# Reordering the first pair of batches in a fused retention and low-rank mixer kernel

## The chip, the core and the metric

The kernel runs on one core of a Trainium2 chip. The metric is the device time of one execution in microseconds (us). The kernel before takes 326.05 us, the median of six runs between 325.9 and 327.28.

## What is computed

First comes a retention layer (attention with decaying weights instead of a softmax), then a mixer on its output: a low-rank mixing over the sequence (U and V) and a two-layer network over the channels (w_ch1 and w_ch2). There are 8 batches, 8 heads, 576 positions, 64 channels per head, 512 channels per position.

```python
scores = scale * np.matmul(q, k.transpose(0, 1, 3, 2))
gamma = 1.0 - 2.0 ** (-5.0 - np.arange(H))
rel = pos[:, None] - pos[None, :]
Dmat = np.where(rel >= 0, gamma[:, None, None] ** rel[None, :, :], 0.0)
attn = np.matmul(scores * Dmat[None], v)
x = attn.transpose(0, 2, 1, 3).reshape(B, S, H * D)
u = x + (x.transpose(0, 2, 1) @ U @ V).transpose(0, 2, 1)
out = u + np.maximum(u @ w_ch1, 0.0) @ w_ch2
```

Inputs and output are float32 in DRAM; the matmuls run in bfloat16.

## The kernel before

Batches go in four pairs. A pair has 2 times 576 positions, which is nine chunks of 128 positions; the chunk in the middle (J, number 4) is half one batch and half the other. The decay is split into a factor on the keys and values and one on the queries or the result, so that within a chunk only a triangular mask is left, and what earlier positions contribute is kept in a running state (keys times values). The mixer then works by batch, on four or five chunks: `MA` (times U), `MH` (times V, added to x, gives u), `MT` (transposes u), Y1 (times w_ch1, ReLU, sixteen items f of 128 hidden channels) and Y2 (times w_ch2, plus u, stored).

Pairs 1 to 3 are worked chunk by chunk in `section`, laid between the Y1 and Y2 matmuls of the batch before by `merge`, which places items by a share of the summed cost. Their queries and keys are transposed by DMA (`xbar`, L279), their staging loads are issued on SyncE by `load` (L243), with 15 staging buffers in rotation.

Pair 0 is worked apart, in an order written out by hand, in `startup` (L909) and `first_stretch` (L1033). The tile framework is told to keep the program order on each engine (`tc.manual_schedule()`), so each engine does its instructions in the order in which these functions emit them, and waits by semaphores. Here the positions are taken in four units of 256 (units 0 and 1 are batch 0, units 2 and 3 are batch 1) and two half chunks J of 64 positions (`hj[0]` and `hj[1]`). The steps are:

- `load_u` (L605) and `load_J` (L792) load on SyncE; `zero_J` (L781) clears staging buffers of the half chunks first. `scale_u` (L637) and `cast_u` (L630) scale and cast to bfloat16, mostly on GpSimd; `cast_J` (L799) and `prep_vJ` (L814) do this for a half chunk: in the kernel before the keys of half chunk 0 on ScalarE and its queries, which are multiplied by `posJ`, on VectorE.
- `T_u` (L646) and `T_J` (L820) transpose on TensorE against the identity, with copies out of PSUM on ScalarE or VectorE.
- `SC_u` (L675), `SC_off` (L719) and `SC_J` (L836) are the scores of a unit, of the off-diagonal block of unit 0, and of a half chunk. `mask_u` (L690) and `mask_J` (L852) multiply by the mask on VectorE; `SC_off` has its copy on ScalarE (L730).
- `RV_u` (L701), `RV_off` (L733), `RV_J` (L862) multiply by the values. `ST_u` (L760) sums the state into `acc1` or `acc2` in PSUM; `Sblk` (L770) copies it into a slot of `sblk` on ScalarE; `QS_u` (L744) and `QS_J` multiply the queries by it. `XS_u` (L752) writes the result x on VectorE.
- `warm` (L205) runs matmuls on the identity whose result is not used.
- `load_w1` (L212) and `load_w2` (L217) load and cast the weights by DMAs issued on GpSimd. A small memset on VectorE into w2's tile (L1089) holds the eight w2 loads until it is done.

PSUM has one buffer each of the kinds `ps_sc`, `ps_o` and `ps_s`, and three `ps_big`, so that a step also waits for the reader of the tile that had its buffer before.

`early_consts` (L117) makes masks, positions and the identity. `first_stretch` lays single Y1 items of batch 0 (`y(1)`) between the steps of units 2 and 3.

Of the kernel before, what the change touches and what calls it, by code (L numbers as in the profile page):

```python
# [34 lines left out]
def kernel(  # L35
# [81 lines left out]
    def early_consts():  # L117
        scratch = y1_pool.tile([P, NF, 4 * P], BF16, tag="y10", name="y1")
        un[0]["off"] = scratch[:, 0:4, :].rearrange("p (a x) (y i) -> p a (x y) i", x=2, i=P)
        tri = scratch[:, 4, 0:P]  # L120
        make_identity(nc, ident)
        nc.gpsimd.memset(lnb, math.log(scale))
        nc.gpsimd.iota(
            posU, pattern=[[2 * P, 4], [1, 2], [0, H]], base=0, channel_multiplier=2,
            allow_small_or_imprecise_dtypes=True,
        )
        nc.gpsimd.iota(
            iotaU, pattern=[[-1, 2], [1, P]], base=0, channel_multiplier=-2,
            allow_small_or_imprecise_dtypes=True,
        )  # L130
# [13 lines left out]
        for h in range(H):  # L144
            nc.vector.memset(lngt[:, :, h], lng[h])
        nc.scalar.activation(out=Af[:, 0, 0:H], in_=lngt[:, 0, :], func=AF.Exp)
        nc.vector.tensor_copy(out=fan, in_=ident[0:R, None, 0:R].to_broadcast([R, 4, R]))
        nc.vector.tensor_scalar_add(posU[:, 2:4], posU[:, 2:4], -float(4 * P - HALF))
        nc.vector.tensor_tensor(
            out=posU.rearrange("p u j h -> p (u j) h"),  # L150
            in0=lngt[:, 0:8, :], in1=posU.rearrange("p u j h -> p (u j) h"), op=ALU.mult)
        nc.scalar.activation(out=vscaleU, in_=posU, func=AF.Exp, bias=lnb, scale=-1.0)
        nc.vector.tensor_scalar(
            out=posJ, in0=posJ, scalar1=0.5, scalar2=None, op0=ALU.mult)
        nc.vector.tensor_tensor(out=posJ, in0=posJ, in1=lngt[:, 0:2, :], op=ALU.mult)
        nc.scalar.activation(out=vscaleJ, in_=posJ, func=AF.Exp, bias=lnb, scale=-1.0)
        nc.scalar.activation(out=posJ, in_=posJ, func=AF.Exp, bias=0.0, scale=1.0)
        nc.vector.tensor_scalar(
            out=triU[0:HALF], in0=iotaU[0:HALF], scalar1=0.0, scalar2=None, op0=ALU.is_ge)
        nc.vector.tensor_scalar(  # L160
            out=triU[HALF:P], in0=iotaU[HALF:P], scalar1=-float(P), scalar2=None,
            op0=ALU.is_ge)
        nc.vector.tensor_scalar_add(pos[:, J + 1:NI, :], pos[:, J + 1:NI, :], -float(S))
        nc.vector.tensor_scalar_add(pos[HALF:P, J, :], pos[HALF:P, J, :], -float(S))
        nc.vector.tensor_tensor(out=lngt, in0=lngt, in1=pos, op=ALU.mult)
        nc.scalar.activation(out=qscale, in_=lngt, func=AF.Exp, bias=0.0, scale=1.0)
        nc.scalar.activation(out=vscale, in_=lngt, func=AF.Exp, bias=lnb, scale=-1.0)
        nc.vector.tensor_copy(out=triH[0:HALF], in_=tri[0:HALF, 0:HALF])
        nc.vector.tensor_copy(out=triH[HALF:P], in_=tri[HALF:P, HALF:P])
        nc.vector.memset(U_E[:, J, :], 0.0)  # L170
        nc.vector.memset(U_O[0:HALF, 0, :], 0.0)
        nc.vector.memset(V4[:, 0:HALF], 0.0)
        nc.vector.memset(V4[:, HALF + S:], 0.0)
        nc.vector.tensor_copy(out=swap[:, 0:HALF], in_=ident[:, HALF:P])
        nc.vector.tensor_copy(out=swap[:, HALF:P], in_=ident[:, 0:HALF])

    def load_u_rows():
        nc.sync.dma_start(
# [53 lines left out]

    ch = {}

    def load(pr, i, which):
        c = ch.setdefault((pr, i), {})
        for j in which:
            if ("f", j) not in c:
                c["f", j] = stage.tile([P, H, D], FP32, tag="stage", name="stage_t")
            dram = (q, k, v)[j]  # L240
            for rows, b, t0 in parts(pr, i):
                n = rows.stop - rows.start
                nc.sync.dma_start(  # L243
                    out=c["f", j][rows, :, :],
                    in_=dram[b, :, t0:t0 + n, :].rearrange("h s d -> s h d"),
                )
# [534 lines left out]
    def zero_J(x, eng):  # L781
        for j in range(3):
            t = stage.tile([P, H, D], FP32, tag="stage", name="stage_t")
            hj[x]["f", j] = t
            if eng is nc.scalar:
                nc.scalar.activation(
                    out=t.rearrange("p h d -> p (h d)"),
                    in_=ident[:, None, :].to_broadcast([P, 4, P]), func=AF.Copy, scale=0.0)
            else:
                eng.memset(t, 0.0)  # L790
# [6 lines left out]
                out=hj[x]["f", j][0:P:2], in_=src.rearrange("h s d -> s h d"))  # L797

    def cast_J(x, eng_k, eng_q):  # L799
        t = qk_pool.tile([P, 2, dm], BF16, tag="qk", name="qk")  # L800
        hj[x]["qk"] = t
        for j, e in ((1, eng_k), (0, eng_q)):
            f = hj[x]["f", j]
            if j == 0 and x == 0:
                e.tensor_tensor(
                    out=t[:, 0, :].rearrange("p (h d) -> p h d", d=D), in0=f,
                    in1=posJ[:, 0, :, None].to_broadcast([P, H, D]), op=ALU.mult)
            elif e is nc.scalar:
                nc.scalar.activation(
                    out=t[:, j, :], in_=f.rearrange("p h d -> p (h d)"), func=AF.Copy)  # L810
            else:
                e.tensor_copy(out=t[:, j, :], in_=f.rearrange("p h d -> p (h d)"))
# [96 lines left out]
    def startup():  # L909
# [12 lines left out]
        cast_unit(0)  # L922
        T_u(0, 1, nc.vector)
        nc.vector.memset(un[0]["off"][HI], 0.0)
        zero_J(1, nc.vector)
        load_J(1, (1, 0, 2))
        load_u(2, (1, 0, 2))
# [7 lines left out]
        cast_unit(1)  # L935
        cast_u(0, 2, 0, nc.gpsimd)
        cast_u(0, 2, 1, nc.gpsimd)
        cast_u(1, 2, 0, nc.gpsimd)
        load_w1(0, 2)
        cast_u(1, 2, 1, nc.gpsimd)  # L940
        T_u(1, 1, nc.scalar)
        SC_u(0, 1, ps_o, "po")
        mask_u(0, 1)
        SC_off(0, ps_sc, "psc")
        warm(3)
        T_u(1, 0)
        nc.vector.memset(sblk, 0.0)
        SC_off(1, ps_o, "po")
        warm(3)
        SC_u(1, 0, ps_sc, "psc")  # L950
        mask_u(1, 0)
        cast_J(0, nc.scalar, nc.vector)
        SC_u(1, 1, ps_o, "po")
        mask_u(1, 1)

        acc1 = pss_tile()
        ST_u(0, ALL, acc1, True)
        Sblk(acc1, 1)
        RV_u(0, 0)
        RV_u(0, 1)  # L960
        RV_off()
        XS_u(0)
        T_J(0)
        acc2 = ps_big.tile([P, NHP, P], FP32, tag="big", name="pss2")
        ST_u(0, ALL, acc2, True)
        prep_vJ(0)
        cast_urows()
        RV_u(1, 0)
        SC_J(0)
        mask_J(0)  # L970
        ST_u(1, LO, acc1, False)
        Sblk(acc1, 2)
        cast_J(1, nc.gpsimd, nc.gpsimd)
        load_w1(2, 4)
        prep_vJ(1)
        load_w1(4, 6)
        scale_u(2, 0, nc.gpsimd)
# [4 lines left out]
        load_w1(8, 10)  # L982
        for hh in range(2):
            cast_u(2, 2, hh, nc.gpsimd)
        load_w1(10, 14)
        scale_u(3, 0, nc.gpsimd)
        for hh in range(2):
            cast_u(3, 0, hh, nc.gpsimd)
        load_w1(14, 16)
        for hh in range(2):  # L990
            cast_u(3, 2, hh, nc.gpsimd)
        RV_u(1, 1)
        QS_u(1, 0, 1)
        XS_u(1, 0, 1)
        ST_u(1, ALL, acc2, False)
        Sblk(acc2, 3)
        QS_u(1, 1, 2)
        XS_u(1, 1, 2)
        RV_J(0)
# [33 lines left out]
    def first_stretch():  # L1033
# [3 lines left out]
        def y(n):  # L1037
            for _ in range(n):
                fn = next(ys, None)
                if fn is not None:  # L1040
                    fn()
# [13 lines left out]

        def unit(u, slots, last):
            T_u(u, 1, nc.vector)
            if last:
                y(1)
            T_u(u, 0)  # L1060
            y(1)
            SC_u(u, 0, ps_sc, "psc")
# [19 lines left out]
            XS_u(u)  # L1082

        for g in range(NI, NI + 4):
            load(*order[g], (1, 0, 2) if g < NI + 3 else (1, 0))
        unit(2, (0, 1, 2), False)
        y(2)
        unit(3, (2, 3), True)
        nc.vector.memset(w2_sb[:, 0, 0:1], 0.0)  # L1089
        for f in range(0, NF, 2):  # L1090
            load_w2(f)
        y(1)
        MA1()
# [1 line left out]
        MH1(outs1[0])  # L1095
        y(2)
        MT1(outs1[0])
        MH1(outs1[1])
        y(16)
        Y1, rest = y1_items(1, by_seg=True)  # L1100
# [68 lines left out]
```

## Time and profile before

| what | value |
|---|---|
| median of six runs | 326.05 us |
| the profiled execution | 325.9 us |
| its span, first to last instruction | 324.1 us |
| TensorE busy | 313.6 us, 97% of the span |
| VectorE, ScalarE, GpSimd busy | 174.0, 145.7, 101.3 us |
| granted TensorE clock | 0.999 |
| bytes moved | 53.3 MB, mean 164 GB/s |
| first Y1 matmul (L515) starts | 24.57 us |
| first transpose by DMA for pair 1 issued, landed | 60.27, 66.98 us |

The profile is of one execution. PE is TensorE, PEld its weight loads, DVE is VectorE, ACT is ScalarE, POOL is GpSimd, SP is SyncE, which only issues DMAs here. In the table of the span in 40 slices (8.1 us each) a digit is the busy share of a slice in tenths. The DMA share is the summed time of packets over 16 engines; since packets of two queues overlap in it, it can be above 1. A row of the timeline has the start, the duration, the engine, the line, the operation and its tiles, the count, and in brackets the idle time before it and what ended it. A line of waits has the total in us, the number of times, and the longest. Ends of matmuls are modelled, so the distance between starts of matmuls is the better measure.

### The profile page before, as it was taken

The page shows a single profiled execution, that of the slowest core. Times are in us where ns is not written, and L with a number is a line of the kernel's source. Part 1 is how long each engine was busy: PE and PEld are TensorE (multiplying, and loading weights), DVE is VectorE, ACT ScalarE, POOL GpSimd, SP SyncE. Part 2 cuts the span into 40 slices and gives each one's busy share as a digit, 9 for nine tenths or more (in the row PEclk, how much of TensorE's full clock was granted, in tenths as well). Part 3 has the DMA queues.
Part 4 walks back from the last instruction along what each step waited for, and adds up shares of the span by engine and source line. Part 5 has one row for each costly group of instructions (what it writes and reads, how often), then busy time and mean ns, then how long its engine had stood idle before and what let it go on. Part 6 is the DMA issues. An engine that isn't in the chain of part 4 may idle for free.

```text
span 324.1 us, 9143 instructions
## 1 busy us (share of the span) xinstructions
PE 313.6 (97%) x3885; PEld 171.2 (53%) x3885; DVE 174.0 (54%) x342; ACT 145.7 (45%) x334; POOL 101.3 (31%) x172
## 2 busy tenths in 40 slices
PE   8899989999999999999999999999999999999996
PEld 3575545764444444457644454457644444467544
DVE  7866546229725577556844476556744475500012
ACT  6757547892020474058800583058800572047400
POOL 7797239222113722052221523052231500010000
PEclk9999999999999999999999999999999999999999
DMA  8999989989975999969997599859997360330022
GB/s 210 262 239 260 237 183 196 208 171 126 256 187 135 244 194 186 211 155 184 192 207 159 140 188 204 215 139 179 191 214 162 97 67 4 106 106 0 2 78 84
DMA packets 152904, 53.30 MB, mean 164 GB/s; under 512 B 132032, under 2 KB 150336, under 8 KB 152864
## 3 DMA queue, kind: packets, MB, share of 16 engines
q1 hardware_dynamic: 144512, 40.40, 68.8%
q0 software_dynamic: 8352, 12.32, 15.6%
q8 instruction: 30, 0.49, 0.7%
q14 instruction: 10, 0.08, 0.1%
HBM read 36.85 MB, written 9.44 MB: 143 GB/s over the span
## 4 chain that ended last, share of the span: by engine, by line
PE 75%; ACT 4%; DMA 3%; DVE 2%; issue 1%; DVEq 0%
PE ps_y L549 35%; PE ps_y L515 32%; DMA qkT<-qk 3%; PE pp L296 2%; DVE u L464 2%; ACT y L520 2%; PE pp L316 1%; PE ps_y L560 1%; PE pp L328 1%; PE AB L358 1%; PE pa L431 1%; PE ph L458 1%; ACT s_sb L373 1%; ACT qk L264 0%; ACT uT L489 0%
## 5 line engine op out<-in xcount | busy, mean ns | idle before, releaser
L515 PE MATMUL ps_y<-uT,w_sb 128*128 128x256 bf16 (+2 forms) x768 | 133.1, 326 | 1.7 <-ACT y L520 1.0
L520 ACT ACTIVATE y<-ps_y 128x384 bf16<-128x384 f32 (+2 forms) x192 | 89.6, 490 | 96.9 <-PE ps_y L515 96.0
L549 PE MATMUL ps_y<-w_sb,y 128*128 128x512 bf16 x560 | 126.5, 380 | 0.0
L515 PEld LDWEIGHTS <-w_sb 128*128 128x128 bf16 x768 | 72.3, 98 | 49.6 <-issue 3.8
L549 PEld LDWEIGHTS <-y 128*128 128x128 bf16 x560 | 52.5, 98 | 61.2
L272 POOL TENSOR_TENSOR vt<-stage_t,vscale 64x256 bf16<-64x256 f32 (+1 forms) x81 | 50.1, 619 | 63.6 <-DMA stage_t<-in_v_dram 49.5
L538 DVE TENSOR_TENSOR o_sb<-ps_y,u 128x512 f32<-128x512 f32 (+2 forms) x38 | 25.2, 664 | 81.7 <-PE ps_y L549 79.3
L541 POOL DMA_DIRECT2D out_dram<-o_sb x31 | 17.1, 553 | 104.7 <-DVE o_sb L538 100.9
L304 DVE TENSOR_TENSOR ret<-pp,triH 128x512 bf16<-128x512 f32 x27 | 18.7, 692 | 23.4 <-PE pp L328 18.0
L464 DVE TENSOR_TENSOR u<-ph,xt 128x768 bf16<-128x768 f32 (+2 forms) x24 | 21.8, 950 | 5.9 <-PE ph L458 4.2
L437 ACT ACTIVATE a_sb<-pa 128x128 bf16<-128x128 f32 x8 | 2.2, 277 | 43.8 <-PE pa L431 43.8
L338 DVE COPY q<-qkT 64x256 bf16<-64x256 bf16 x48 | 14.2, 297 | 14.0 <-DMA qkT<-qk 13.1
L344 DVE TENSOR_TENSOR xt<-pp,qscale 128x512 bf16<-128x512 f32 x27 | 18.6, 689 | 4.7 <-PE pp L328 4.2
L263 DVE CAST qk<-stage_t 64x256 bf16<-64x256 f32 x54 | 18.8, 347 | 1.2
L383 DVE TENSOR_TENSOR s_sb<-AB,Af 64x256 bf16<-64x256 f32 x42 | 17.7, 422 | 2.1 <-ACT s_sb L378 1.5
L264 ACT ACTIVATE qk<-stage_t 128x512 bf16<-128x512 f32 x27 | 16.8, 622 | 0.0
L635 POOL CAST qk<-stage_t 128x512 bf16<-128x512 f32 x16 | 10.6, 660 | 10.8 <-DMA stage_t<-in_v_dram 5.3
L376 ACT ACTIVATE Af<-AB 128x256 f32<-128x256 f32 x24 | 9.2, 384 | 8.2 <-PE AB L358 7.7
L692 DVE TENSOR_TENSOR ret<-psc,triU 128x1024 bf16<-128x1024 f32 x8 | 9.6, 1206 | 3.9 <-PE psc L684 3.9
L296 PEld LDWEIGHTS <-qkT 64*64 64x64 bf16 x432 | 5.6, 107 | 10.4 <-issue 7.8
L261 ACT ACTIVATE qk<-stage_t 128x256 bf16<-128x256 f32 x27 | 11.1, 410 | 0.0
L209 PE MATMUL pw<-ident 128*128 128x512 bf16 x26 | 8.6, 477 | 1.4 <-POOL ident masks.py:199 1.4
(134 smaller groups left out, 220.1 us busy)
## 6 DMA issues: line engine op xcount, KB each, us to landing
stage_t<-in_k_dram SPq DMA_DIRECT2D x32, 256.0 KB, 4.7
stage_t<-in_q_dram SPq DMA_DIRECT2D x32, 256.0 KB, 5.5
stage_t<-in_v_dram SPq DMA_DIRECT2D x32, 256.0 KB, 5.6
out_dram<-o_sb POOLq DMA_DIRECT2D x31, 256.0 KB, 3.5
w_sb<-in_moe_w_ch_dram POOLq DMA_DIRECT2D x14, 256.0 KB, 8.1
stage_t<-in_k_dram SPq DMA_DIRECT2D x8, 128.0 KB, 3.8
stage_t<-in_q_dram SPq DMA_DIRECT2D x8, 128.0 KB, 3.9
stage_t<-in_v_dram SPq DMA_DIRECT2D x8, 128.0 KB, 4.1
```

Source lines behind the costliest of these rows:

```text
L263: nc.vector.tensor_copy(out=o[to, hl], in_=f[fr, hl])
L264: nc.scalar.activation(out=c["qk"][:, 0, :], in_=c["f", 0].rearrange("p h d -> p (h d)"), func=AF.Copy)
L272: nc.gpsimd.tensor_tensor(out=o[to, hl], in0=f[fr, hl], in1=w[fr, hl, :, None].to_broadcast([n, NHP, D]), op=ALU.mult)
L304: nc.vector.tensor_tensor(out=ret.rearrange("p a b i -> p a (b i)").rearrange("p a (b i) -> p a b i", i=D), in0=pp[:, :, 0:NHP * D].rearra ...
L344: nc.vector.tensor_tensor(out=st["x", pr][:, i, :].rearrange("p (hp hl d) -> p hl hp d", hl=2, d=D), in0=pp[:, :, NHP * D:2 * NHP * D].rea ...
L383: nc.vector.tensor_tensor(out=S_[half(x), 1, :], in0=Bk[half(1 - x)], in1=Af[half(1 - x), now, :], op=ALU.add)
L464: nc.vector.tensor_tensor(out=st["u", par][:, i0 - base:i0 - base + n, w].rearrange("p s (c d) -> p c s d", c=2), in0=ph[k][:, :, 0:n, :], ...
L515: nc.tensor.matmul(ps[:, 0:n, :], w1_sb[:, cc, f * P:(f + 1) * P], st["uT", par][:, c0:c0 + n, cc, :], start=(cc == 0), stop=(cc == NCC - 1),)
L520: nc.scalar.activation(out=st["y1", par][:, f, c0 * P:(c0 + n) * P], in_=ps[:, 0:n, :].rearrange("p s t -> p (s t)"), func=AF.Relu)
L538: nc.vector.tensor_tensor(out=o_sb[:, 0:n], in0=ps[:, 0:n], in1=st["u", par][:, c, w], op=ALU.add)
L541: (nc.sync if last else nc.gpsimd).dma_start(out=out_flat[r0:r0 + P, w], in_=o_sb[:, 0:n])
L549: nc.tensor.matmul(ps, st["y1", par][:, f, c * P:(c + 1) * P], w2_sb[:, f, :], start=(f == 0), stop=(f == NF - 1),)
```

## The change

In `early_consts` the copies that make `triH` and `swap` go from VectorE to ScalarE, and are placed earlier; the memset of `sblk` comes in here from `startup`; four small memsets go from here to `startup`, behind the memset of the off block.

In `startup` the half chunk's queries are scaled on GpSimd, between the value casts of unit 0 and those of unit 1; its keys are cast on ScalarE behind the second off block. One of the two `warm(3)` goes. The state sums `ST_u` are emitted earlier, the two masks of unit 1 follow one another on VectorE without the query scaling between, and `T_J(0)` stands ahead of `RV_u(0, ...)`. On GpSimd, the w1 columns 2 to 4 are loaded before the casts of half chunk 1; the columns 10 to 14 behind the query casts of unit 3; and a memset into the staging tile of pair 1's first keys, behind the last w1 load, holds their load on SyncE.

In `first_stretch` a Y1 item goes from behind unit 2 to between its two transposes, and the w2 loads are issued in two groups of four, the second behind a memset on VectorE that follows the first part of `MH1` and `MT1`.

```diff
@@ early_consts
+        nc.scalar.activation(out=triH[0:HALF], in_=tri[0:HALF, 0:HALF], func=AF.Copy)
+        nc.scalar.activation(out=triH[HALF:P], in_=tri[HALF:P, HALF:P], func=AF.Copy)
+        nc.scalar.activation(out=swap[:, 0:HALF], in_=ident[:, HALF:P], func=AF.Copy)
+        nc.scalar.activation(out=swap[:, HALF:P], in_=ident[:, 0:HALF], func=AF.Copy)
...
-        nc.vector.tensor_copy(out=triH[0:HALF], in_=tri[0:HALF, 0:HALF])
-        nc.vector.tensor_copy(out=triH[HALF:P], in_=tri[HALF:P, HALF:P])
-        nc.vector.memset(U_E[:, J, :], 0.0)
-        nc.vector.memset(U_O[0:HALF, 0, :], 0.0)
-        nc.vector.memset(V4[:, 0:HALF], 0.0)
-        nc.vector.memset(V4[:, HALF + S:], 0.0)
-        nc.vector.tensor_copy(out=swap[:, 0:HALF], in_=ident[:, HALF:P])
-        nc.vector.tensor_copy(out=swap[:, HALF:P], in_=ident[:, 0:HALF])
+        nc.vector.memset(sblk, 0.0)
@@ load
-    def load(pr, i, which):
+    def load(pr, i, which, gate=None):
...
+            if gate is not None:
+                gate.memset(c["f", j][:, 0:1, 0:1], 0.0)
@@ startup
         nc.vector.memset(un[0]["off"][HI], 0.0)
+        nc.vector.memset(U_E[:, J, :], 0.0)
+        nc.vector.memset(U_O[0:HALF, 0, :], 0.0)
+        nc.vector.memset(V4[:, 0:HALF], 0.0)
+        nc.vector.memset(V4[:, HALF + S:], 0.0)
         zero_J(1, nc.vector)
...
         cast_u(0, 2, 1, nc.gpsimd)
+        cast_J(0, None, nc.gpsimd)
         cast_u(1, 2, 0, nc.gpsimd)
+        cast_u(1, 2, 1, nc.gpsimd)
         load_w1(0, 2)
-        cast_u(1, 2, 1, nc.gpsimd)
         T_u(1, 1, nc.scalar)
...
         T_u(1, 0)
-        nc.vector.memset(sblk, 0.0)
         SC_off(1, ps_o, "po")
-        warm(3)
+        cast_J(0, nc.scalar, None)
         SC_u(1, 0, ps_sc, "psc")
         mask_u(1, 0)
-        cast_J(0, nc.scalar, nc.vector)
-        SC_u(1, 1, ps_o, "po")
-        mask_u(1, 1)
-
         acc1 = pss_tile()
         ST_u(0, ALL, acc1, True)
         Sblk(acc1, 1)
+        SC_u(1, 1, ps_o, "po")
+        mask_u(1, 1)
+        acc2 = ps_big.tile([P, NHP, P], FP32, tag="big", name="pss2")
+        ST_u(0, ALL, acc2, True)
+
+        T_J(0)
         RV_u(0, 0)
         RV_u(0, 1)
+        ST_u(1, LO, acc1, False)
         RV_off()
+        Sblk(acc1, 2)
         XS_u(0)
-        T_J(0)
-        acc2 = ps_big.tile([P, NHP, P], FP32, tag="big", name="pss2")
-        ST_u(0, ALL, acc2, True)
         prep_vJ(0)
         cast_urows()
-        RV_u(1, 0)
+        load_w1(2, 4)
         SC_J(0)
         mask_J(0)
-        ST_u(1, LO, acc1, False)
-        Sblk(acc1, 2)
+        ST_u(1, ALL, acc2, False)
+        Sblk(acc2, 3)
+        RV_u(1, 0)
         cast_J(1, nc.gpsimd, nc.gpsimd)
-        load_w1(2, 4)
         prep_vJ(1)
...
-        load_w1(10, 14)
         scale_u(3, 0, nc.gpsimd)
         for hh in range(2):
             cast_u(3, 0, hh, nc.gpsimd)
+        load_w1(10, 14)
         load_w1(14, 16)
+        load(*order[NI], (1,), gate=nc.gpsimd)
         for hh in range(2):
             cast_u(3, 2, hh, nc.gpsimd)
...
-        ST_u(1, ALL, acc2, False)
-        Sblk(acc2, 3)
@@ first_stretch
             T_u(u, 1, nc.vector)
-            if last:
-                y(1)
+            y(1)
             T_u(u, 0)
...
         unit(2, (0, 1, 2), False)
-        y(2)
+        y(1)
         unit(3, (2, 3), True)
         nc.vector.memset(w2_sb[:, 0, 0:1], 0.0)
-        for f in range(0, NF, 2):
+        for f in range(0, NF // 2, 2):
             load_w2(f)
...
         MT1(outs1[0])
+        nc.vector.memset(w2_sb[:, NF // 2, 0:1], 0.0)
+        for f in range(NF // 2, NF, 2):
+            load_w2(f)
```

More of the change, by code (lines that the diff above doesn't have):

```diff
@@ L799, in cast_J @@
     def cast_J(x, eng_k, eng_q):
-        t = qk_pool.tile([P, 2, dm], BF16, tag="qk", name="qk")
-        hj[x]["qk"] = t
+        if "qk" not in hj[x]:
+            hj[x]["qk"] = qk_pool.tile([P, 2, dm], BF16, tag="qk", name="qk")
+        t = hj[x]["qk"]
         for j, e in ((1, eng_k), (0, eng_q)):
+            if e is None:
+                continue
             f = hj[x]["f", j]
@@ L1084, in first_stretch @@
         for g in range(NI, NI + 4):
-            load(*order[g], (1, 0, 2) if g < NI + 3 else (1, 0))
+            load(*order[g], ((0, 2) if g == NI else (1, 0, 2)) if g < NI + 3 else (1, 0))
         unit(2, (0, 1, 2), False)
-        y(2)
+        y(1)
         unit(3, (2, 3), True)
         nc.vector.memset(w2_sb[:, 0, 0:1], 0.0)
-        for f in range(0, NF, 2):
+        for f in range(0, NF // 2, 2):
             load_w2(f)
```

## The prediction

> **What bounds the kernel now.** I read the page first, then busy time by stretch, then the waits of TensorE, then the timeline of the first 80 us with the landing times of single DMAs, and the chain that ended last. Times are us from the start of the span.
>
> ```profile
> PE 313.6 (97%) x3885; PEld 171.2 (53%) x3885; DVE 174.0 (54%) x342; ACT 145.7 (45%) x334; POOL 101.3 (31%) x172
> PE   8899989999999999999999999999999999999996
> DMA  8999989989975999969997599859997360330022
> ```
>
> TensorE is at 97%, so only what delays TensorE counts. From slice 11 on it is full, and none of that code changes. All edits lie before 67 us. There the DMA row is as full as the PE row:
>
> ```profile
> 20.00:40.00 20.00, 18.89 (x263) 11.52 (x263) 11.55 (x17) 13.36 (x29) 11.75 (x17) 1.00 1.25 259
> 40.00:46.00 6.00, 5.32 (x95) 3.03 (x94) 3.44 (x4) 1.99 (x5) 1.22 (x2) 1.00 0.82 167
> 46.00:66.00 20.00, 19.32 (x187) 12.27 (x180) 7.81 (x14) 15.87 (x35) 11.18 (x17) 1.00 1.19 197
> 78.00:100.00 22.00, 22.00 (x271) 10.27 (x269) 13.62 (x25) 2.30 (x6) 3.32 (x7) 1.00 0.94 191
> ```
>
> The columns are PE, PEld, DVE, ACT, POOL, clock, DMA share, GB/s. Until 66 us the DMA engines are loaded above 1 except at 40 to 46, and TensorE misses 0.7 to 1.1 us in each stretch. After 78 us it misses nothing. The waits of TensorE in 0 to 25 and 25 to 85 us:
>
> ```profile
> PE psx L726 <- DVE ret L692: 0.6, 1, 0.6
> PE po L711 <- DVE ret L692: 0.5, 1, 0.5
> PE po L746 <- DVE xt L754: 0.3, 1, 0.3
> PE pss L763 <- POOL qk L635: 0.7, 2, 0.4
> PE pp L296 <- DMA qkT<-qk: 0.4, 2, 0.2
> ```
>
> So the start waits for VectorE; unit 3 waits for its values; pair 1 waits for the transposes of its first chunks. The rows behind that:
>
> ```profile
> 5.07 1.04 DVE L168 COPY triH<-y 64x64 bf16<-64x64 bf16 x1
> 10.61 2.29 DVE L692 TENSOR_TENSOR ret<-psc,triU 128x1024 bf16<-128x1024 f32 x2
> 13.71 0.82 PE L209 MATMUL pw<-ident 128*128 128x512 bf16 x3
> 16.25 0.71 DVE L805 TENSOR_TENSOR qk<-stage_t,posJ 128x512 bf16<-128x512 f32 x1
> 16.39 0.64 PE L711 MATMUL po<-qk,ret 64*128 64x64 bf16 x32 [0.52 <-DVE ret L692]
> 30.04 0.74 POOL L214 DMA_DIRECT2D w_sb<-in_moe_w_ch_dram x1
> 40.29 1.32 POOL L635 CAST qk<-stage_t 128x512 bf16<-128x512 f32 x2 [2.27 <-DMA stage_t<-in_v_dram]
> 71.72 5.01 DMA qkT<-qk
> 76.78 0.32 PE pp L296 x16
> ```
>
> The last two are from the chain: it passes through the third chunk's transpose, landed at 76.73. After that it is matmuls. So the change is worth what it moves the matmul at 76.78, no more.
>
> **The start.** VectorE loses the two triH copies (1.04 and 0.54) and two swap copies (0.2) to ScalarE. That engine sat idle 1.89 us before L166, and four copies at some 0.25 each fit: no cost there. The 0.91 sblk memset takes their place at 5.15, done by 6.1; the copy of unit 0's transposed keys, at 7.09, can start when those transposes end, about 6.6. If the memset were drawn out by a GpSimd operation (1.05) that gain is gone, not more. The small memsets (0.4 together) now stand behind the off-block memset, so the three staging memsets end near 10.3 instead of 10.68, and the first mask starts at 10.3 instead of 10.61: the off block of L726 gains 0.3. Its unit then runs to the end of the second off block at 13.3. The removed three warm-up matmuls held TensorE from 13.71 to 14.46 (0.75); the scores of L684 now wait for the copies of the transposed queries (13.9). Gain 0.55.
>
> Scaling the half chunk's queries moves from VectorE (0.71) to GpSimd, where the same shape takes 1.04 (L816). Its data landed at 13.89 (8.95 plus 4.9), so it ends at 14.95, needed at 15.6. Behind it on GpSimd are the casts of unit 1's values: the second now ends near 16.7, and L763 for acc1, pulled forward, needs it at 16.65. Cost 0.1. Also behind: the first w1 load, issued 16.7 instead of 15.4, landing 4.6 later at 21.3, needed at 23.9: 2.6 to spare. The second w1 load now goes ahead of the casts of half chunk 1 (19.1 instead of 20.1); those end near 21.1 instead of 20.2, and its values near 22.15 instead of 22.0, needed by L826 at 23.1 and L894 at 26: nothing, with 2 us of cover. VectorE now has its masks in a row: ends 15.5 and 16.7 instead of 16.3 and 18.1. Key cast on ScalarE: 14.4 to 15.0, ahead of L773 for acc1 (its input is ready at 14.8, its output wanted at 18.8), so nothing.
>
> The new order of TensorE to the second L746, summed from spacings in the trace: scores 13.9, acc1 14.3, scores 14.8, acc2 15.2, transposes 15.6, L711 16.05, acc1 16.7, L737 17.2, half-chunk scores 17.65, acc2 17.75, L711 18.2. There VectorE decides: L754 from 17.75 (1.21), L856 (0.76), L754 (0.69) end at 20.35. L746 starts at 20.4 instead of 21.08. Lead: 0.7, carried to the first L515 (24.57 becomes 23.9). Bounds 0.3 and 1.0.
>
> **Units 2 and 3.** One Y1 item goes from behind unit 2 into it. It fills the 0.34 wait at 28.54, but brings f4 to 29.8, while its w1 columns land at 30.4 (21.95 plus 8.4). Net loss 0.3, so the lead is 0.4. The 512 KB w1 load is moved from 30.04 behind unit 3's query casts, and the next k load, with all that follows on SP, is held by a memset on GpSimd behind both last w1 loads (31.5 becomes about 37). Unit 3's values landed at 40.2 and 40.9; without the 512 KB ahead they come by about 38. The two gaps of TensorE at L763 (0.73 and 0.54 between starts, 0.27 of it needed) give back 1.0: lead 1.4.
>
> The price is that f10 now needs that w1 load at 42.32 minus 1.4 = 40.9, and it is issued near 35.6. In this trace it took 10.7 us: landing 46.3, a stall of 5.4. The Trainium skill (DMA: Bandwidth & Descriptors, Anatomy of one DMA) states 2 us plus bytes at 436 GB/s for such a DMA: an estimate of 3.2, landing 38.8, no stall. Neither fits: the row had a backlog of four loads on both queues, the page has none. Nearest is the first pair of w2 loads, together 512 KB: issued at 46.92 into a GpSimd queue that was empty, while SP was loading; the second landed 6.7 after the first's issue. With SP held for a while I take 6.2: 41.8, a stall of 0.9. Lead 0.5; bounds minus 4.0 and 1.4.
>
> The hold on SP has a price of its own. The same page (Issuing engines are not separate DMA queues) says all queues run on the same 16 engines and interleave, so by it a hold costs nothing as long as either queue has work. The rows say the share is 1.25 with both queues loaded, and 1.15 at 2 to 14 us with SP alone, 0.82 at 40 to 46. One queue alone for some 3 us would lose 0.1 by 3 = 0.3; against that, the hole at 40 to 46 (6 times 0.37 = 2.2 below the earlier share) partly fills, as the held loads run there. I take a gain of 0.3 from it for the transposes, bounds minus 1.5 and 1.5.
>
> **w2 in two groups.** The second memset stands behind the first pair of L464, which ends at 50.17; four issues from 46.92 (0.73 each) end at 49.8. So group two is held 0.4, while only one w2 load has landed (4.4): its queue never runs dry. Cost and gain nothing. GpSimd behind it has L272 at 52.5, early enough.
>
> **Does the lead reach 76.78?** The transposes stand on SP behind k and q loads that land at 65.0 and 66.0, just after the last w2 (51.79 plus 12.8 = 64.6). These are starved by w2, and w2 starts when unit 3 is done. If unit 3 is 0.5 earlier, w2 and what follows are, too. Sum: 0.5 plus 0.3 = 0.8 of the profiled 325.9 (its span is 324.1, the remaining 1.8 lies around it): 325.1, and from the median of 326.05: 325.2.
>
> **The rivals.**
> Swallowed: the transposes land when the DMA engines have moved everything, with no regard to TensorE. For: share above 1 for 20 us before them, waits of 0.2 at L296. Then TensorE waits 0.7 more there, and the time is 326.1.
> Late w1 (the slower side): the 512 KB load is late for f10. It decides from a landing beyond 42.3, a latency of 6.7. For: 8.1 median for w1 and w2 loads, 10.7 for this one. Against: few loads ahead of it. At 8.1 it lands at 43.7, 1.4 behind the old start: 327.4.
> All gaps close: the start gives 1.0, f10 doesn't stall, and the transposes come early, so that lead 1.4 and part of the waits at 66 to 77 (0.8) come off: 324.0.
>
> **How the numbers follow.** About 0.2% (0.65 us) is what a measurement can tell from no change. Forecast 0.46 (0.34 beyond 0.65, 0.12 within); swallowed 0.20 (0.17 within, 0.03 slower); late w1 0.24, slower; all gaps 0.10, faster. Faster 0.44, same 0.29, slower 0.27. The forecast's own range is 324.6 to 325.8; for 8 in 10 it reaches nearly to the all-gaps time and to the late w1: 323.9 to 327.4.
>
> **What would show it.** Start: L746's second group at 20.4, first L515 at 23.9; L692's masks back to back. Units: no wait of L763 on POOL after 38; L515's item f10 near 41.8, and a wait of PEld on the w1 DMA before it if it was late. L296 at 66.3 and 76.0. I am wrong if f10 starts after 42.3, or if L296 waits over 0.5 for qkT.

## The result: slower by 0.5%

The changed kernel takes 327.89 us (median of 17 runs, 327.12 to 329.26) against 326.21 us for the kernel before, run beside it (median of 38, 324.48 to 327.75). The ratio is 1.0054, with an interval of 1.0041 to 1.0067: 1.7 us slower, where 0.8 us faster was forecast, and outside the range given. The profiled execution of the changed kernel took 328.08 us with a span of 326.3, 2.2 more than the 324.1 of before. Line numbers in the changed kernel are lower by 1 to 3: L514 is Y1, L548 Y2, L295 pair 1's scores, L745 the queries times the state, L753 the result x, L683 the scores of a unit.

The page's busy times and the rows of slices, in the same form as shown for before:

```profile
PE 313.4 (96%) x3882; PEld 171.2 (52%) x3882; DVE 171.4 (53%) x338; ACT 146.7 (45%) x338; POOL 102.3 (31%) x174
PE   7889989979999999999999999999999999999996
DMA  8999799997994999969998599968998440340012
```

TensorE does the same work, but for three unused matmuls, in a longer span. Three of its digits are one lower than before: the first, the third (16 to 24 us) and the ninth (65 to 73 us). The first two cost nothing, since the first Y1 matmul still starts earlier than before; the loss arises in the ninth. The same stretches as before, and two more (columns PE, PEld, DVE, ACT, POOL, clock, DMA share, GB/s):

```profile
20.00:40.00 20.00, 18.56 (x253) 11.06 (x253) 12.24 (x17) 11.97 (x25) 13.00 (x20) 1.00 1.05 225
40.00:46.00 6.00, 4.96 (x93) 2.89 (x93) 3.28 (x4) 2.24 (x5) 0.00 (x0) 1.00 1.30 220
46.00:66.00 20.00, 19.36 (x177) 12.34 (x177) 7.81 (x15) 15.74 (x35) 9.63 (x15) 1.00 1.20 205
68.00:72.00 4.00, 3.56 (x36) 2.08 (x37) 1.71 (x5) 2.01 (x5) 1.80 (x3) 0.63 1.05 211
70.00:72.00 2.00, 2.00 (x9) 1.14 (x8) 0.22 (x1) 0.96 (x3) 1.80 (x3) 0.50 1.15 207
78.00:100.00 22.00, 22.00 (x331) 10.46 (x330) 12.96 (x27) 2.69 (x7) 2.80 (x5) 1.00 0.90 181
```

From 20 to 40 us the DMA engines moved 225 GB/s instead of 259, a loss of 0.68 MB; from 40 to 46 they moved 220 instead of 167, which returns 0.32. At 68 to 72 the granted clock is 0.63, and within it, at 70 to 72, 0.50. TensorE's waits, the first two from 0 to 25 us, the others from 25 to 85:

```profile
PE po L745 <- DVE xt L753: 1.0, 1, 1.0
PE psc L683 <- DVE qkT L664: 0.6, 1, 0.6
PE pp L295 <- DMA qkT<-qk: 1.9, 1, 1.9
PE ps_y L514 <- DMA w_sb<-in_moe_w_ch_dram: 1.0, 1, 1.0
```

Of the waits shown before, those for the masks are smaller or gone, and that of L763 for unit 3's values is gone. The wait for the result x (L746, here L745) has grown from 0.3 to 1.0, and one of 0.6 for the transposed queries is new (L683). Later come 1.0 for the late w1 load and, decisive, 1.9 for the first transpose of pair 1 (0.4 before, in two waits). The timeline's rows behind them:

```profile
14.67 2.36 DVE L691 TENSOR_TENSOR ret<-psc,triU 128x1024 bf16<-128x1024 f32 x2 [0.61 <-PE psc L683]
18.22 1.23 DVE L753 TENSOR_TENSOR xt<-po,qscale 128x1024 bf16<-128x1024 f32 x1 [1.19 <-PE po L736]
20.76 0.40 PE L745 MATMUL po<-sblk,qkT 128*128 128x128 bf16 x4 [0.97 <-DVE xt L753]
36.48 1.55 POOL L211 DMA_DIRECT2D w_sb<-in_moe_w_ch_dram  x2
38.05 1.18 POOL L634 CAST qk<-stage_t 128x512 bf16<-128x512 f32 x2
38.16 0.37 SPq L242 DMA_DIRECT2D stage_t<-in_k_dram  x1
42.07 1.04 PE L514 MATMUL ps_y<-uT,w_sb 128*128 128x512 bf16 x4 [0.99 <-DMA w_sb<-in_moe_w_ch_dram]
68.44 0.32 PE L295 MATMUL pp<-qkT 64*64 64x64 bf16 x16 [1.89 <-DMA qkT<-qk]
```

Two lines of the chain that ended last:

```profile
64.65 3.75 DMA qkT<-qk
68.89 6.12 PE ps_y L514 x32
```

and, from the kernel before, the row of the same first scores:

```profile
67.03 0.32 PE L296 MATMUL pp<-qkT 64*64 64x64 bf16 x16 [0.23 <-DMA qkT<-qk]
```

Follow the lead down the rows. The first Y1 matmul starts at 24.26 instead of 24.57, and item f10 at 42.07 instead of 42.32, so up to 42 us the changed kernel is ahead by some 0.3. The first transpose is issued at 64.65 instead of 60.27 and lands at 68.40 instead of 66.98: TensorE's first scores of pair 1 are now 1.41 behind (68.44 against 67.03). The next two sets of scores start at 74.94 and 79.13 instead of 72.36 and 76.78, which is 2.6 and 2.4 behind, and the span ends 2.2 later. The 1.2 that came on top between the first and the second set goes with the half clock, at which the Y1 matmuls there ran in part.

Why the transpose is late is read from the DMA queues between 36 and 42 us (queue, packets, MB, share of 16 engines; q1 carries SyncE's loads, q0 GpSimd's). Before:

```profile
DMA packets 3362, 1.23 MB, mean 205 GB/s; under 512 B 2286, under 2 KB 3360, under 8 KB 3360
q1 hardware_dynamic: 2690, 0.79, 58.6%
q0 software_dynamic: 670, 0.42, 48.0%
```

and after, with the rows of 40 slices of 0.15 us each:

```profile
DMA  1111000000000478499938999999999999999999
GB/s 34 38 34 41 20 20 24 20 20 24 20 3 0 68 68 89 68 89 89 75 61 150 184 198 184 177 198 212 184 205 191 218 205 205 178 177 181 167 208 232
DMA packets 833, 0.68 MB, mean 114 GB/s; under 512 B 26, under 2 KB 832, under 8 KB 832
q0 software_dynamic: 740, 0.63, 74.8%
q1 hardware_dynamic: 92, 0.04, 2.6%
```

First there is next to nothing to move. From 36.6 to 37.95 us the share is below a tenth, at 24 GB/s and less: SyncE's last load was issued at 30.68 and only its tail is left, and the w1 loads, issued from 36.48, have no packets under way yet. Then only w1 flows. The held key load is issued at 38.16, yet from 38 to 42 us GpSimd's queue moves 732 packets and SyncE's 6:

```profile
q0 software_dynamic: 732, 0.63, 111.3%
q1 hardware_dynamic: 6, 0.00, 0.3%
```

The held load lands at 44.86. What SyncE's queue moved in 30 to 48 us, before and after, and in 30 to 66 us, before and after:

```profile
q1 hardware_dynamic: 8453, 2.55, 61.1%
q1 hardware_dynamic: 6534, 2.09, 54.0%
q1 hardware_dynamic: 13918, 3.93, 55.5%
q1 hardware_dynamic: 12673, 3.63, 51.5%
```

By 48 us it is 0.46 MB behind, by 66 still 0.30, which at the 212 GB/s of the 66 to 72 us stretch is an estimated 1.4 us. Pair 1's fourth query load, the last one issued ahead of the transpose, lands 1.40 later (67.44 instead of 66.04), and the transpose 1.42.

### The profile page after: what moved, and what is told of

Its sections match the earlier page's. It is cut to its first block, busy times and chain, and to the rows that moved or that the text cites. A ratio compares the mean times of both kernels' runs of the same rounds, so it can differ in the third digit from the quotient of the medians.

```text
span 326.3 us, 9129 instructions
## 1 busy us (share of the span) xinstructions
PE 313.4 (96%) x3882; PEld 171.2 (52%) x3882; DVE 171.4 (53%) x338; ACT 146.7 (45%) x338; POOL 102.3 (31%) x174
## 4 chain that ended last, share of the span: by engine, by line
PE 77%; ACT 3%; DMA 3%; DVE 2%; issue 1%; DVEq 0%
PE ps_y L548 36%; PE ps_y L514 32%; DMA qkT<-qk 3%; DVE u L463 2%; PE pp L295 2%; PE pp L315 1%; ACT y L519 1%; PE ps_y L559 1%; PE pp L327 1%; PE AB L357 1%; PE pa L430 1%; PE ph L457 1%; ACT s_sb L372 0%; ACT uT L488 0%; ACT qk L263 0%
## 5 line engine op out<-in xcount | busy, mean ns | idle before, releaser
L514 PE MATMUL ps_y<-uT,w_sb 128*128 128x256 bf16 (+2 forms) x768 | 134.8, 329 | 2.3 <-DMA w_sb<-in_moe_w_ch_dram 1.0
L548 PE MATMUL ps_y<-w_sb,y 128*128 128x512 bf16 x560 | 126.5, 380 | 0.0
L514 PEld LDWEIGHTS <-w_sb 128*128 128x128 bf16 x768 | 72.9, 99 | 50.8 <-issue 4.3
L548 PEld LDWEIGHTS <-y 128*128 128x128 bf16 x560 | 52.5, 98 | 61.2
L295 PEld LDWEIGHTS <-qkT 64*64 64x64 bf16 x432 | 5.6, 107 | 11.7 <-issue 8.5
L295 PE MATMUL pp<-qkT 64*64 64x64 bf16 x432 | 8.6, 198 | 2.3 <-DMA qkT<-qk 2.3
```

What stands on the lines that cost most here:

```text
L295: nc.tensor.matmul(pp[half(m), m ^ hl, hp * D:(hp + 1) * D], qkT[half(hl), NHP + hp, half(m)], qkT[half(hl), hp, half(m ^ hl)], start=True ...
L514: nc.tensor.matmul(ps[:, 0:n, :], w1_sb[:, cc, f * P:(f + 1) * P], st["uT", par][:, c0:c0 + n, cc, :], start=(cc == 0), stop=(cc == NCC - 1),)
L548: nc.tensor.matmul(ps, st["y1", par][:, f, c * P:(c + 1) * P], w2_sb[:, f, :], start=(f == 0), stop=(f == NF - 1),)
```

## The experiments

Each ratio is to the kernel before, timed beside it, with its interval in brackets; an interval that holds 1 means that no difference is shown. "First transpose" is the landing of pair 1's first; it, waits and starts come from one profiled execution each, which need not be a typical one.

**The changed kernel without the hold.**

```diff
-        load(*order[NI], (1,), gate=nc.gpsimd)
...
-            load(*order[g], ((0, 2) if g == NI else (1, 0, 2)) if g < NI + 3 else (1, 0))
+            load(*order[g], (1, 0, 2) if g < NI + 3 else (1, 0))
```

> The changed kernel without the memset that holds SyncE: the keys of pair 1's first chunk are loaded as in the kernel before; the rest of the change stays. Theory hold (SyncE's queue ran dry while it was held, so that everything behind it, the transposes at L278 included, came later): no load-free stretch of SyncE's queue at 36 to 42 us, the first transpose lands by 67.0 instead of 68.4, TensorE's 1.9 us wait at L295 goes, and the time falls by 1.3 to 2.0, to about 326.2. Rival w1 (the stall of 1.0 for the late 512 KB w1 load is what costs): the stall stays or grows to 2, the time stays above 327.5. Rival w2 (two groups): the same, above 327.5.

Measured: 1.0007 [0.9980, 1.0034], first transpose 67.64. SyncE's queue in 36 to 42 us, and TensorE's waits:

```profile
q1 hardware_dynamic: 2047, 0.55, 45.0%
PE ps_y L514 <- DMA w_sb<-in_moe_w_ch_dram: 1.4, 1, 1.4
PE pp L295 <- DMA qkT<-qk: 0.6, 2, 0.4
```

Most of the loss goes with the hold, although f10 now waits 0.4 longer for w1. The 512 KB w1 load took 6.0 us here, from issue to landing.

**The same, and the 512 KB w1 load back ahead of unit 3's query casts.**

```diff
+        load_w1(10, 14)
         scale_u(3, 0, nc.gpsimd)
...
-        load_w1(10, 14)
         load_w1(14, 16)
```

> As the one without the hold, and the 512 KB w1 load is back ahead of unit 3's keys, where it was. Theory hold: TensorE's stall of 1.0 for w1 goes, at most 0.7 comes back as the wait of L762 for unit 3's values; 325.6 to 326.2, so level with the kernel before or up to 0.6 under it. Rival w1: only now does the loss go, by 1.0 to 1.7 against the run without the hold alone.

Measured: 1.0016 [0.9993, 1.0039]. This run couldn't tell the late load's cost from nothing. The stall at f10 is gone in its profiled execution, but that one waited 1.5 for unit 3's queries, which wasn't expected, and twice 0.8 for w1 columns of early items (at 25.36 and 29.14 us).

**The changed kernel with w2 in one group.**

```diff
-        for f in range(0, NF // 2, 2):
+        for f in range(0, NF, 2):
             load_w2(f)
...
-        nc.vector.memset(w2_sb[:, NF // 2, 0:1], 0.0)
-        for f in range(NF // 2, NF, 2):
-            load_w2(f)
```

> The changed kernel with all eight w2 loads issued in one group behind the first memset, as before. Theory hold: no effect, within 0.4 of the changed kernel (327.9), since the second group was held 0.75 us while the first was still moving. Rival w2: the loss goes, 326.2 to 327.0.

Measured: 1.0060 [1.0039, 1.0080], first transpose 69.77, L295 waits 3.5 in all. The loss stays without the two groups, so they are not its cause.

**The kernel before with the hold alone.**

```diff
         load_w1(14, 16)
+        load(*order[NI], (1,), gate=nc.gpsimd)
...
-            load(*order[g], (1, 0, 2) if g < NI + 3 else (1, 0))
+            load(*order[g], ((0, 2) if g == NI else (1, 0, 2)) if g < NI + 3 else (1, 0))
```

> The kernel before with only the hold added: the keys of pair 1's first chunk wait for a memset on GpSimd behind the last w1 load. The 512 KB w1 load stays ahead of unit 3. Theory hold: slower by 1.0 to 2.0, so 327.2 to 328.2, with a wait of 1 to 2 at L296. Rival w1: within 0.4 of the kernel before, since no w1 load is late.

Measured: 1.0019 [0.9994, 1.0043], first transpose 68.27 (66.98 in before), the held load issued at 38.30. The queues between 36 and 42 us and the waits:

```profile
q1 hardware_dynamic: 1568, 0.42, 31.3%
PE pp L298 <- DMA qkT<-qk: 1.7, 3, 0.7
```

The direction is that of the theory, but the interval holds 1, and the loss of 0.6 between the medians is below the 1.0 to 2.0 that were expected.

**The changed kernel again**, as a control on the chip of the next three.

> The changed kernel again, on the chip of the runs beside it. It should be 0.4 to 0.7% above the kernel before, as in the result, with a wait of TensorE at L295 of 1.5 to 3 us, and a granted clock of 0.995 in about two thirds of its executions.

Measured: 1.0050 [1.0024, 1.0075], first transpose 70.58, L295 waits 3.9 in all, f10 starts at 42.56. The loss repeats, with the same two waits, the first of them longer than expected. The clock of 0.995 or less came in five of its twelve executions, fewer than expected.

**The kernel before with the hold and the late w1 load.**

```diff
-        load_w1(10, 14)
...
+        load_w1(10, 14)
         load_w1(14, 16)
+        load(*order[NI], (1,), gate=nc.gpsimd)
```

> The kernel before with two edits: the hold on SyncE and the 512 KB w1 load behind unit 3's query casts. Theory pair (the hold costs most when the late w1 load takes the DMA engines just as SyncE comes back): slower by 0.4 to 0.8%, the first held load lands 6.5 or more after its issue, the wait at L295's counterpart (L298 here) is over 1.5. Rival (the two add up without regard to one another, or the cost lies in the start): 0.1 to 0.3%.

Measured: 1.0034 [1.0012, 1.0056], first transpose 69.87, q1 0.05 MB in 36 to 42.

```profile
PE pp L298 <- DMA qkT<-qk: 3.1, 2, 2.5
PE ps_y L517 <- DMA w_sb<-in_moe_w_ch_dram: 1.1, 1, 1.1
```

These two edits on the kernel before make the two waits of the changed kernel, and a loss that is clear of zero, but smaller than the theory's 0.4 to 0.8%. The empty stretch of SyncE's queue is there too.

**The kernel before with the start's edits alone** (all of `early_consts`, `cast_J` and `startup` but for the hold and the place of the 512 KB load). Its core:

```diff
+        cast_J(0, None, nc.gpsimd)
         cast_u(1, 2, 0, nc.gpsimd)
...
-        warm(3)
+        cast_J(0, nc.scalar, None)
         SC_u(1, 0, ps_sc, "psc")
         mask_u(1, 0)
-        cast_J(0, nc.scalar, nc.vector)
...
+        T_J(0)
         RV_u(0, 0)
```

> The kernel before with the changes ahead of unit 2 alone: ScalarE copies, memsets, half-chunk queries on GpSimd, the order of state sums, masks and values, one warm-up less. No hold, w1 and w2 and the Y1 items as before. Theory of the prediction: 0.3 to 0.7 us earlier at the first Y1 matmul. If that reaches the end: 0.1 to 0.2% faster than before. Rival swallowed (the transposes land when the DMA engines are through): level, within 0.1%.

Measured: 0.9979 [0.9962, 0.9996], first Y1 matmul at 24.27. It is repeated in two groups below.

**The changed kernel with eight unused matmuls ahead of pair 1's first scores**, to keep TensorE busy while it waits.

```diff
-            [(0.04, ready(0)), (0.05, fetch(3, (2,))), (0.06, fetch(4, (1, 0))),
+            [(0.204, lambda: warm(8)), (0.04, ready(0)), (0.05, fetch(3, (2,))), (0.06, fetch(4, (1, 0))),
```

> The changed kernel with eight warm-up matmuls, whose result is not used, put ahead of the first scores of pair 1, where TensorE otherwise waits 1.9 us for the transpose. Theory clock (the idle stretch costs the full clock for 3.4 us after it): the clock stays 1.0, the spacing of the matmuls at L514 behind the wait goes back from 6.1 to 5.0 us, and the time falls by 0.4 to 1.2 against the changed kernel. Rival (the clock falls for other reasons, or costs nothing because the next transposes are late anyway): the same time or up to 0.4 more.

Measured: 1.0072 [1.0047, 1.0097]. In the profiled execution the clock stayed at 1.00 from 64 to 76 us, but in four of the six runs its mean was still 0.995, with a median of 329.99 us. The filler did not help, against the theory; it shows neither that the idle time causes the clock's drop nor that it doesn't.

**The kernel before with the late w1 load alone.**

```diff
-        load_w1(10, 14)
...
+        load_w1(10, 14)
         load_w1(14, 16)
```

> The kernel before with one part of the change alone: the 512 KB load of w1 stands behind the query casts of unit 3; nothing else differs, no hold on SyncE. Theory (hold and late load add up, the hold starving SyncE's queue and the late load stalling f10): the late load alone costs its own stall, f10 waits 0.3 to 1.2 us, but the loads on SyncE, which run through, get its bandwidth, so pair 1's first transpose lands at 67 to 67.6 us and the time is 0 to 0.15% above before. Rival (the late load is the whole loss, the hold does nothing): ratio 1.003 to 1.005, as with both edits together.

Measured: 1.0018 [0.9997, 1.0039], first transpose 68.48, later than the 67 to 67.6 expected. The timeline's row of f10:

```profile
44.65 1.89 PE L515 MATMUL ps_y<-uT,w_sb 128*128 128x512 bf16 x4 [3.27 <-DMA w_sb<-in_moe_w_ch_dram]
```

The expectation missed the size of the stall: 3.3 instead of 0.3 to 1.2. This execution, at 330.13 us, is one of the slowest of its run (median 327.57), so the size isn't typical either. With SyncE's loads running beside it the w1 load takes 7.4 us from issue to landing, and 6.0 in the changed kernel without the hold; behind the hold it took 5.4 to 5.6 in five profiles. So the hold shortens that load by 0.4 to 2 us in these profiles, and pays for it with SyncE's loads. Ratios of the two alone (+0.19% and +0.18%) add up to that of both (+0.34%), within intervals of 0.2%.

**The hold alone, made longer**: the memset stands behind unit 3's value casts (the diff is to the kernel with the hold alone).

```diff
-        load(*order[NI], (1,), gate=nc.gpsimd)
         for hh in range(2):
             cast_u(3, 2, hh, nc.gpsimd)
+        load(*order[NI], (1,), gate=nc.gpsimd)
```

> The kernel before with the hold on SyncE alone, made longer: the memset that holds pair 1's first key load stands behind unit 3's value casts on GpSimd, near 41.7 us instead of 38.3. Theory (an empty SyncE queue is lost transfer time, which comes back at pair 1's transposes): the first transpose lands 1.5 to 3.5 us later than with the short hold (68.3), at 70 to 72, TensorE waits 3 to 5 us more at pair 1's scores, and the time is 0.6 to 1.3% above before. Rival (the queues share one pool, what SyncE loses GpSimd's loads gain, and the transposes land when all bytes are through): w2 and the rest come earlier by the same, first transpose by 68.5, ratio under 1.003.

Measured: 1.0054 [1.0034, 1.0075]. The held load is issued at 41.98. Queues in 36 to 42 us, then the wait:

```profile
DMA  9999999999999977333255979999999983212111
q1 hardware_dynamic: 593, 0.29, 21.5%
PE pp L298 <- DMA qkT<-qk: 2.7, 2, 1.7
```

With the hold as the only edit, 3.7 us more of it make a loss that is clear of zero and of the rival's bound (1.003). The first transpose landed at 68.78, earlier than the theory had it (70 to 72), and the waits are 2.7, not 3 to 5. The profiled execution, at 327.88 us against a median of 328.79, shows a part of the loss only.

**The start's edits alone, with half of the w2 loads held until pair 1's first chunk is cast.**

```diff
+        def w2_rest():
+            nc.vector.memset(w2_sb[:, NF // 2, 0:1], 0.0)
+            for f in range(NF // 2, NF, 2):
+                load_w2(f)
...
-            [(0.04, ready(0)), (0.05, fetch(3, (2,))), (0.06, fetch(4, (1, 0))),
+            [(0.04, ready(0)), (0.045, w2_rest), (0.05, fetch(3, (2,))), (0.06, fetch(4, (1, 0))),
```

> The kernel before with the start's edits alone, as in the run with only these, and the second half of the w2 loads held until VectorE has cast pair 1's first chunk, near 59.5 us instead of 50. Theory (TensorE's waits at 66 to 77 us come from k and q loads of pair 1 that are starved by w2, so a megabyte less ahead of them lets the first transpose land 3 to 4 us earlier): first transpose landed by 64.5, the waits at pair 1's first two scores (0.4 to 1.2 us) gone, w2's last load landed by 71, before it is needed at 76; ratio to before 0.994 to 0.997. Rival (the start's gain is what there is; the transposes wait for their place on SyncE, not for bytes): first transpose at 66.5 to 68, ratio 0.998 as without this edit, or above 1.000 if the second group comes late for w2's use.

Measured: 1.0029 [1.0003, 1.0054]. Issues on SyncE, GpSimd's w2 issues, and TensorE's wait:

```profile
60.28 1.34 SPq L278 DMA_TRANSPOSE qkT<-qk  x1
58.04 2.92 POOL L215 DMA_DIRECT2D w_sb<-in_moe_w_ch_dram  x4 [6.27 <-DVE w_sb L1124]
PE pp L295 <- DMA qkT<-qk: 2.4, 1, 2.4
```

Both theories fail here. The query load ahead of the transpose did land early (61.99), but the four w2 loads issued from 58.04 then ran beside the transpose, which took 8.86 us and landed at 69.14. So, in this one profile, what GpSimd's queue held at that moment counted for the transpose too.

**The start's edits alone, again.**

> The kernel before with the start's edits alone, again, beside the others on one chip. Both theories: ratio 0.996 to 0.9995 (0.9979 the first time), first Y1 matmul at 24.2 to 24.35 us, waits at pair 1's first scores of 0.4 to 1.2 us in all.

Measured: 0.9988 [0.9965, 1.0012].

**One more group on one chip, for the two small edits:** the start's edits alone, with the moved Y1 item, with the two w2 groups, and with both (the last is the changed kernel without hold and late load, measured above at 1.0016). The two edits:

```diff
             T_u(u, 1, nc.vector)
-            if last:
-                y(1)
+            y(1)
...
-        y(2)
+        y(1)
         unit(3, (2, 3), True)
...
-        for f in range(0, NF, 2):
+        for f in range(0, NF // 2, 2):
             load_w2(f)
...
+        nc.vector.memset(w2_sb[:, NF // 2, 0:1], 0.0)
+        for f in range(NF // 2, NF, 2):
+            load_w2(f)
```

> The base of this group: the kernel before with the start's edits alone. Expected by both theories at 0.997 to 0.9995 of before (0.9979 and 0.9988 in two runs).

> The start's edits and the Y1 item that is moved into unit 2. Theory (the moved item meets its w1 columns before they have landed, a wait of up to 0.8 us on the w1 DMA near 29 us, as in the run without the hold and the late load): ratio 0.3 to 0.8 us above the base, 0.998 to 1.001, with a wait on w1 of 0.3 to 0.9 us before 31 us. Rival (it fills a wait for unit 2's queries and costs nothing): as the base within 0.1%.

> The start's edits and w2 in two groups. Theory (the second memset holds four loads under 1 us behind a queue that still has work): as the base within 0.1%, last w2 load landed near 64.6 to 65.5 us. Rival (the groups shift the packets that pair 1's loads and first transpose get, so they cost what is missing between the base and the run with Y1 and w2 edits, 1 us): ratio 1.000 to 1.003, first transpose landed 1 us later than in the base.

> The start's edits, the moved Y1 item and w2 in two groups, again, which is the changed kernel without the hold and the late load (1.0016 to before in another group of runs). Theory (each small edit costs what it costs alone): the sum of the two single edits, 0.998 to 1.002. Rival (the difference between the groups was chip to chip): as the base within 0.1%.

Measured, in this order: 0.9999 [0.9982, 1.0016], 1.0003 [0.9977, 1.0030], 0.9994 [0.9972, 1.0017] and 0.9996 [0.9976, 1.0016]. Neither edit costs anything that can be seen, and no wait of 0.3 to 0.9 for w1 showed up with the moved item; between the 1.0016 and the 0.9996 of the same kernel no difference is shown. None of the four is distinguishable from the kernel before either. Only the start's edits were once below 1 with their whole interval, and two repeats didn't confirm it.

## Why the prediction was wrong

**The step that failed** is "The hold on SP has a price of its own", which ended in "I take a gain of 0.3 from it for the transposes, bounds minus 1.5 and 1.5". It was a loss of 1.4 at the first transpose (68.40 against 66.98), so close to the lower bound, and 2.1 off the forecast, which had L296 at 66.3 and got 68.44. Two premises were wrong. The first was that one queue alone runs at a share of 1.15, so that some 3 us would cost 0.1 each. SyncE was not alone with work; it was the one without, and GpSimd's queue too moved nothing for 1.35 us, because the same change had taken its 512 KB load from 30.04 to 36.48 (with the hold alone on the kernel before, 36 to 42 us still moved 1.07 MB, with both edits 0.55). The share at 36 to 42 us was 0.78, against 1.08 before, and the hold lasted until 38.16 instead of 37. The second was that the hole at 40 to 46 would be filled by the held loads. It was filled (1.30 instead of 0.82), but with w1 until 42, and that was less than had been lost: 0.46 MB of SyncE's loads were missing at 48 us and 0.30 at 66. (The hole had been sized from the wrong row, too: 0.37 is its distance from the later share of 1.19; from the earlier 1.25 it is 0.43.) The Trainium skill's sentence (DMA: Bandwidth & Descriptors, Issuing engines are not separate DMA queues) that DMAs of all engines interleave was rightly not taken for the sum. The 6 packets against 732 from 38 to 42 us don't agree with it; from 48 to 66 us, with work in both queues, they did share (49.0% and 69.5% of the 16 engines' time).

That this made the loss is shown by the experiments: the changed kernel without the hold is at 1.0007 [0.9980, 1.0034] instead of 1.0050 to 1.0060, hold and late load alone on the kernel before are at 1.0034, and a longer hold alone is at 1.0054. The path from the hold to the time is less firm, since it rests on one profile for each run. In 36 to 42 us the seven profiles with a hold moved 0.55 to 1.07 MB, the eleven without it 1.10 to 1.39 but for 0.86 with the late load alone. The first transpose landed at 68.27 to 70.58 with the hold, at 65.9 to 69.3 without: later on the whole, but the ranges overlap, so the 1.42 of one pair of profiles is within what profiles without a hold differ by.

By the prediction's own test ("if L296 waits over 0.5 for qkT") it was wrong at 1.9.

**"Does the lead reach 76.78?"** failed with it. "If unit 3 is 0.5 earlier, w2 and what follows are, too": w2 started 0.24 earlier (46.68), but SyncE's loads were behind for another reason. The rival Swallowed had the right place, the transposes, and took the wrong lateness: it kept them where they were. A rival in which the hold itself makes them later was missing, though the bound of minus 1.5 contained it; with a landing 1.4 later the same sum gives 327.5 from the median. The rival Late w1 had a time that was nearly right, 327.4, but for a reason that didn't hold: its load was not late enough (below).

**The start** was right in kind, and the forecast of it too large: 0.31 instead of 0.7. Y1 began at 24.26, not 23.9, and L745's second group at 20.76, not 20.4. The term that was mis-sized is the gain at the scores behind the removed warm-up, 0.55: they started at 14.21, not 13.9, as they wait for VectorE's copy of the transposed queries (0.6 in the row of L683), a gain of 0.25. VectorE's masks stood back to back as predicted, but L736, which now stands behind the half chunk's transposes and one more state sum, let L753 begin at 18.22, later than the 18.01 of before. Over three groups the start's edits gave 0.9979, 0.9988 and 0.9999.

**Units 2 and 3.** The lead of 0.4 after the moved Y1 item was hit by luck: f4 did not wait for its columns (they had landed at 29.7, it started at 30.30), so that the lead grew by 0.1 to 0.42 at f9 instead of shrinking by 0.3, and the two errors cancel. No wait for the values after 38: right. The late w1 load: latency 5.5 instead of 6.2, and f10 waited 1.0 instead of 0.9, at 42.07 instead of 41.8. This is right, in part through the hold: without it the load took 6.0 and the stall was 1.4 in the changed kernel, and 7.4 and 3.3 with the late load alone, which is the rival Late w1. **The two w2 groups** cost nothing (held 0.75 instead of 0.4), as predicted.

**What wasn't foreseen** is the half clock behind the wait: 6.50 us from the first to the second scores of pair 1 instead of 5.33, so 1.2 us more in the profiled execution. In 13 of the 19 executions on record (two more than the 17 of the median) the mean clock was 0.993 to 0.995, with a median of 328.28 us; the other six, at 0.999 or 1.000, had 327.52. So some 0.8 between executions goes with the drop, and 1.3 of the loss is there without it. The drop isn't peculiar to the hold: 7 of the 14 executions of the changed kernel without the hold had a mean of 0.995 or less.

**Still open:** the hold costs the changed kernel 0.4 to 0.5% and the kernel before 0.19%. In the first, the late load stands ahead of the held ones, and q1 moved 0.04, 0.10, 0.16 and, with the filler, 0.34 MB in 36 to 42 us; in the second it moved 0.42. That could make such a difference, but the run with 0.34 had the highest ratio of the four, the intervals overlap, and the start's gain of 0.1% with the 0.34% of hold and late load leave 0.3% of the 0.54% not attributed to one edit.

## What to carry to other kernels

Before you hold a queue's loads back to let others pass, look at what is then left to move, above all if the same change has moved the others' loads away. The stretch in which the DMA share dropped was lost here, and the loss came back where the last transfer of that queue was waited for, 30 us later. Price a hold in bytes (what its queue moved in that stretch, less what is won back by the time of the wait, by the rate there), not by the share of an average stretch. And when you move loads later, see that they don't land beside a transfer that the critical engine waits for: in the one run here that did so, the transfer took 8.86 us.

## What the runs showed of the hardware

- When a load was issued on SyncE (38.16) behind w1 loads of GpSimd's queue, SyncE's queue moved 6 packets from 38 to 42 us, and the load took 6.70 us; with GpSimd's queue nearly drained (the longer hold, 41.98) a load of the same 256 KB took 3.19.
- A transpose by DMA took 3.75 us in the changed kernel, issued when the last w2 load had landed, 6.71 in the kernel before, issued while w2 was still moving, and 8.86 with four w2 loads issued in the 3 us around its own issue.
- The granted clock fell to 0.5 for 3.41 us (0.63 in the 68 to 72 us row) behind a wait of 1.9 us. With the late w1 load alone it fell behind a wait of 3.3: four Y1 matmuls took 1.89 us instead of 1.04. In the run with half of w2 held it fell behind a wait of 2.4 (0.89 in 66 to 72 us). The Trainium skill (TensorE: Matmul & The Clock Gate, Why this matters for your kernels) warns of gaps over about 3 us; here it fell behind one of 1.9, while in the control a wait of 3.6 left the profiled clock at 1.00. So the length of the wait alone doesn't decide it.
